# The end of a weight stream: last modes in another bank, last Z in two halves, first U laid later

## The chip, the cores and the metric

The kernel runs on one core of a Trainium2 chip. The metric is the device time of one execution in microseconds (us), the median of several runs. TensorE (PE) multiplies, with its weight loads (PEld) shown apart; VectorE (DVE), ScalarE (ACT) and GpSimd (POOL) work on elements; SyncE (SP), ScalarE and GpSimd issue transfers (DMA). Products land in PSUM, which the program hands out in banks of 512 float32 a partition, and have to be copied to SBUF from there.

## What is computed

Eight batches of 576 positions with eight heads of 64 go through a masked attention (four heads local, four strided). Its result x, of 576 rows by 512 features, goes through a mixing step in the frequency domain and a channel product with a rectifier:

```python
X = np.fft.rfft(x, axis=1)
Xr, Xi = np.real(X[:, :n_modes]), np.imag(X[:, :n_modes])      # n_modes = 64
Yr = np.einsum('bmd,mde->bme', Xr, w_r) - np.einsum('bmd,mde->bme', Xi, w_i)
Yi = np.einsum('bmd,mde->bme', Xr, w_i) + np.einsum('bmd,mde->bme', Xi, w_r)
Y[:, :n_modes] = Yr + 1j * Yi
u = x + np.fft.irfft(Y, n=S, axis=1)
return u + np.maximum(u @ w_ch, 0.0)
```

The weights w_r and w_i are 64 matrices each of 512 by 512 float32. They are by far the most of what is read.

## The kernel before

**Stages.** The program's order is written out by hand: each engine executes its instructions in the order in which the Python code issues them, and the framework adds the waits. First comes the strided half of the attention (up to line 836), then the local half with the first modes (lines 839 to 862), then the rest of the modes of the first half with the channel product of x (lines 893 to 935), then the stage "late" (937 to 1041) and the output stage (1042 to 1082).

**Modes.** A mode m of a half is a 256-row slice of w_r[m] and of w_i[m]: a weight tile of 128 partitions (64 real, 64 imaginary), four row groups c and 512 columns e. `w_fetch` (line 157) fetches two modes at a time through GpSimd's queue, converting float32 to float16. Most pairs are two transfers of 512 KB; the last two pairs are cut by mode, so that each of their transfers carries one mode's real or imaginary half (lines 188 to 190, 256 KB). Each transfer waits for the landing of the eighth transfer before it, and for the modes that held its buffer before.

`mode(slot, m)` (line 614) multiplies. In the last 16 modes (48 to 63 of slot 1) the weights stand still and the spectrum X moves: sixteen small matmuls (line 630, 128x16) a mode, four row groups for each of four column groups e. Eight modes share one PSUM tile `y` (lines 623 and 624). VectorE adds the finished ones to the other half's product Y0 and writes the spectrum tile YT (line 564, `spectrum`): for the last tile after mode 61 (six modes) and after mode 63 (two).

**Between the modes.** In the stage "late", `late[i]` names work that follows the i-th mode of `rest`: `renew` (line 948) adds the inverse transform of the first 96 spectrum rows to v0 (channel product of x) and xo (x itself), through pairs of PSUM banks `p`, three of them in rotation. After mode 62 (`late[22]`, line 1037) come `v_early(0)`, `v_early(1)` and `u_early(0)`: each lays two tiles of v0 or xo into a PSUM pair with a product by the identity `idn` (lines 987 and 992), as the start of an accumulation.

**After the last mode.** Lines 1042 to 1053: `spec_z(3, 0)` multiplies the last 32 spectrum rows (four batches of them) by w_ch into `zp`, four matmuls of 512 columns (line 736); ScalarE copies it to `zzs[0]`; eight transposes give the same rows of Y into `yp`, which VectorE copies to `yys[0]` and `yys[1]`.

**Output stage.** Its 18 items are pairs of output tiles. For item k, `v_early` lays V, `new_rows` (line 1001) adds the last spectrum rows to it, `v_done` (line 1013, ScalarE) takes the Relu into `rl`; `u_early` lays U, `new_rows` adds, and `u_done` (line 1020, VectorE) adds U and `rl` into `osb`, which SP sends out. Item 0 is done in two pieces. The first two items are written out (lines 1056 to 1064); from k = 2 on the loop issues V of item k beside U of item k-1. V, and U of even items, use the pairs `p`; U of odd items the pair `u`. At k = 8 (lines 1066 to 1069) the second half of the last spectrum rows is multiplied into one more of the pairs `p` (`held`) and ScalarE copies it to `zzs[1]`.

## Time and profile before

| | |
|---|---|
| median of three runs | 427.61 us (427.32 to 427.89) |
| profiled execution, span from first to last instruction | 426.7 us |
| PE / PEld busy | 346.4 us (81%) / 208.2 us (49%) |
| DVE / ACT / POOL busy | 234.7 / 218.3 / 110.7 us |
| transfers | 91.62 MB, mean 215 GB/s |
| GpSimd's queue (weights, q, k, v), share of 16 engines' span | 96.2% |
| mean granted TensorE clock | 0.926 |

The profiled execution has no time of its own beside its span; the median of the runs is 0.9 us above it, which is what lies before the first and after the last instruction and the difference between executions.

How to read it: "busy" is the time in which an engine's instructions ran. The page cuts the span into 40 slices and gives for each the busy share of the engines, the granted clock and the transfers' share. The chain that ended last is followed back from the last instruction, at each step to what released it; a stretch of it names what had to be shorter for the end to come earlier. The timeline lists instructions with start, length and, in brackets, how long the engine idled before and what ended that. A matmul's length has a tail in which the next one already runs: matmuls of 512 columns start 0.21 us apart and are listed with 0.38.

### The profile page before, as it was taken

How to read it: one execution, taken by the hardware profiler on the slowest of the kernel's cores; microseconds unless marked ns; L12 is line 12 of the kernel's file. 1: busy time of each engine (PE TensorE's matmuls, PEld its weight loads, DVE VectorE, ACT ScalarE, POOL GpSimd, SP SyncE). 2: the span in 40 equal slices, each digit the busy share in tenths (PEclk: the TensorE clock that was granted, in tenths of full speed). 3: DMA queues.
4: the chain of work that ended last, by engine and by line, in shares of the span. 5: the costliest groups of instructions: out<-in, count | busy, mean ns of one | idle time of the engine just before them, and what ended most of it. 6: DMA issues, size and time to landing. Idle time of an engine off the chain costs nothing.

```text
span 426.7 us, 9768 instructions
## 1 busy us (share of the span) xinstructions
PE 346.4 (81%) x4167; PEld 208.2 (49%) x4167; DVE 234.7 (55%) x466; ACT 218.3 (51%) x390; POOL 110.7 (26%) x196
## 2 busy tenths in 40 slices
PE   2977878769999698889768788878788867889993
PEld 2866767554656365566433344435444423445330
DVE  3788778851355154356113246746676354655884
ACT  1687678643656356556642235423442444443872
POOL 8332333322423222222222322222232222210000
PEclk9999899967999689999995889989999979989997
DMA  8999999999999999999999999999999999995698
GB/s 150 210 212 212 213 213 213 211 211 211 214 213 213 213 213 215 212 214 215 210 214 211 213 214 213 210 213 215 212 213 214 213 213 214 214 212 105 244 355 287
DMA packets 30938, 91.62 MB, mean 215 GB/s; under 512 B 4464, under 2 KB 5232, under 8 KB 30896
## 3 DMA queue, kind: packets, MB, share of 16 engines
q0 software_dynamic: 25168, 81.28, 96.2%
q1 hardware_dynamic: 4976, 9.13, 5.9%
q10 hardware_dynamic: 752, 0.61, 0.5%
q8 instruction: 32, 0.52, 0.5%
q14 instruction: 10, 0.08, 0.0%
HBM read 162.83 MB, written 9.44 MB: 404 GB/s over the span
## 4 chain that ended last, share of the span: by engine, by line
DMA 47%; PE 29%; DVE 14%; ACT 5%; issue 3%; DVEq 0%; POOL 0%; ACTq 0%; POOLq 0%
DMA wt<-in_moe_w_i_dram 38%; DMA wt<-in_moe_w_r_dram 7%; PE y L597 5%; DVE xb L241 3%; DVE kz L283 3%; PE p L987 2%; ACT X L251 2%; PE sc L532 2%; PE tp L413 2%; PE sc L459 1%; PE p L1001 1%; PE y L532 1%; PE p L760 1%; DVE yy L752 1%; DVE rec L240 1%
## 5 line engine op out<-in xcount | busy, mean ns | idle before, releaser
L597 PE MATMUL y<-wt,X 128*32 128x512 f16 (+1 forms) x448 | 70.9, 430 | 20.1 <-DMA wt<-in_moe_w_i_dram 20.1
L186 POOL DMA_DIRECT2D wt<-in_moe_w_r_dram x59 | 34.7, 588 | 126.4 <-PE y L597 56.3
L186 POOL DMA_DIRECT2D wt<-in_moe_w_i_dram x60 | 35.4, 590 | 68.3 <-DMA wt<-in_moe_w_i_dram 44.4
L597 PEld LDWEIGHTS <-X 128*32 128x32 f16 (+1 forms) x448 | 28.1, 140 | 39.4 <-DMA wt<-in_moe_w_i_dram 18.6
L727 DVE COPY xo<-tp 128x512 f16<-128x512 f16 x32 | 22.1, 691 | 36.8 <-PE tp L725 36.8
L726 ACT ACTIVATE v<-sc 128x512 f16<-128x512 f32 x32 | 19.1, 597 | 44.2 <-PE sc L717 44.2
L717 PE MATMUL sc<-w_cp,xT 128*128 128x512 f16 x128 | 36.9, 410 | 1.9 <-DVE xT L690 1.9
L489 ACT ACTIVATE PL<-sc 128x480 f16<-128x480 f32 (+1 forms) x48 | 27.0, 578 | 21.3 <-PE sc L475 21.0
L241 DVE TENSOR_TENSOR xb<-av,rec 90x256 f16<-90x256 f32 (+2 forms) x80 | 36.0, 450 | 2.8
L240 DVE RECIPROCAL rec<-av 90x4 f32<-90x4 f32 (+2 forms) x80 | 14.6, 183 | 39.3 <-PE av L504 28.2
L251 ACT ACTIVATE yr<-y 128x512 f16<-128x512 f32 x28 | 16.7, 597 | 36.8 <-PE y L597 35.6
L961 DVE TENSOR_TENSOR xo<-p,xo 128x1024 f16<-128x1024 f32 x16 | 19.6, 1225 | 21.7 <-PE p L760 21.7
L420 DVE COPY qT<-tp 128x576 f16<-128x576 f16 x16 | 11.9, 752 | 34.7 <-PE tp L413 34.7
L251 ACT ACTIVATE v<-p 128x1024 f16<-128x1024 f32 x16 | 16.4, 1023 | 23.1 <-PE p L760 23.1
L378 ACT ACTIVATE PL<-sc 90x360 f16<-90x360 f32 (+1 forms) x48 | 22.7, 490 | 7.0 <-PE sc L371 6.4
L251 ACT ACTIVATE v<-tp 128x640 f16<-128x640 f16 (+1 forms) x24 | 19.0, 807 | 11.8 <-PE tp L447 9.3
L413 PE MATMUL tp<-cI_s,ring 64*64 64x64 f16 x864 | 22.4, 197 | 2.7 <-DVE qT L420 2.4
L459 PE MATMUL sc<-cMl_s,cI_s 128*128 128x480 f16 (+1 forms) x48 | 19.4, 405 | 4.5 <-ACT PL L489 2.9
L276 PE MATMUL tp<-cI_s,ring 72*128 72x72 f16 x256 | 15.4, 207 | 8.7 <-DMA ring<-in_v_dram 7.1
L413 PEld LDWEIGHTS <-ring 64*64 64x64 f16 x864 | 17.5, 110 | 9.4 <-issue 5.4
L251 ACT ACTIVATE kz<-tp 64x360 f16<-64x360 f16 (+1 forms) x32 | 18.9, 592 | 6.2 <-PE tp L413 5.2
L1013 ACT ACTIVATE rl<-p 128x1024 f32<-128x1024 f32 (+1 forms) x19 | 18.4, 979 | 5.7 <-PE p L1001 3.1
(142 smaller groups left out, 737.9 us busy)
## 6 DMA issues: line engine op xcount, KB each, us to landing
wt<-in_moe_w_i_dram POOLq DMA_DIRECT2D x60, 512.0 KB, 18.8
wt<-in_moe_w_r_dram POOLq DMA_DIRECT2D x59, 512.0 KB, 17.7
out_dram<-osb SPq DMA_DIRECT2D x15, 512.0 KB, 3.4
ring<-in_v_dram POOLq DMA_DIRECT2D x8, 288.0 KB, 13.4
ring<-in_q_dram POOLq DMA_DIRECT2D x8, 288.0 KB, 13.6
ring<-in_k_dram POOLq DMA_DIRECT2D x8, 288.0 KB, 13.1
ring<-in_v_dram POOLq DMA_DIRECT2D x3, 512.0 KB, 14.8
ring<-in_q_dram POOLq DMA_DIRECT2D x3, 512.0 KB, 14.8
```

What stands on the lines that cost most here:

```text
L186: nc.gpsimd.dma_start(dst, rows)
L241: nc.vector.tensor_tensor(out=dst, in0=val.rearrange("p h (q c) -> p h c q", c=4), in1=rec[0:n, 0:pieces] .to_broadcast((n, pieces, 64)) . ...
L251: nc.scalar.activation(out=out, in_=in_, func=ACTF.Copy)
L378: nc.scalar.activation(out=PS[0:n, ds(POFF[t], 4 * n)], in_=scp[0:n, 0 : 4 * n], func=ACTF.Exp, scale=SCALE,)
L413: nc.tensor.transpose(tp[ds(64 * hp, 64), ds(64 * i, 64)], qn[ds(64 * hp, 64), ds(64 * (9 * g + i), 64)], idn[ds(64 * hp, 64), ds(64 * hp, ...
L459: nc.tensor.matmul(scp[:, 0 : n * times].rearrange("p (h x) -> p h x", h=times), idn, mask_rows("cMl", n, times), start=True, stop=False,)
L489: nc.scalar.activation(out=dst, in_=src, func=ACTF.Exp, scale=SCALE)
L597: nc.tensor.matmul(yp[ds(a, 32), :], Xh[half][pr, c].rearrange("p b r (h m) -> p (b r h) m", h=2)[:, :, mm % 32], wt[pr, XC[c], :], start= ...
L717: nc.tensor.matmul(vp, xT[:, ch], w_chs["cp"][:, ch, :], start=(ch == 0), stop=(ch == 3),)
L726: nc.scalar.activation(out=v0, in_=vp, func=ACTF.Copy)
L727: nc.vector.tensor_copy(out=xo.rearrange("p (h q c) -> p h q c", h=2, c=4), in_=tp[:, 0:512].rearrange("p (h c q) -> p h q c", h=2, c=4),)
L961: nc.vector.tensor_tensor(out=xo, in0=up[:, 0:n], in1=xo, op=AluOp.add)
```

## The change

- **Transfers.** The last mode (63) is fetched in four transfers: columns 0 to 1023 of the tile's 2048 (row groups 0 and 1), real and imaginary, then columns 1024 to 2047 (row groups 2 and 3). Each is 128 KB.
- **Bank.** Mode 62 takes a new tile `y`, which modes 62 and 63 share.
- **Last mode by rows.** Mode 63 first opens all its 64 columns with one matmul of the identity by a tile of zeros, then adds its sixteen products sorted by row group: eight that need the first two transfers, eight that need the last two.
- **First V and U.** After mode 62 only `v_early(0)` is left; `v_early(1)` follows mode 63; `u_early(0)` follows the row products of items 0 and 1.
- **Last Z.** The product by w_ch is made in two halves of 256 columns, each in a bank of its own of one pair `p`; ScalarE copies the first, VectorE the second, before the transposes of Y.
- **Pairs.** Instead of a rotating pool of three pairs there are three named ones, and `pair(n)` says which is taken: V by the parity of its item, U of even items the third. `held` at k = 8 and V of item 8 are both `(npair[0] + 0) % 3`. In the row products the order for items 0 and 1 stays; they now stand between the transposes of Y and their copies.

```diff
@@ w_fetch
-                single += [(j, ri, dst[:, j], rows[:, j]) for j in ones]
-            for _, _, to, rows in sorted(single, key=lambda x: x[:2]):
+                for j in ones:
+                    n = 2 * DM if m + j == NM - 1 else 4 * DM
+                    for a in range(0, 4 * DM, n):
+                        single.append(
+                            (j, a, ri, dst[:, j, a : a + n], rows[:, j, a : a + n])
+                        )
+            for *_, to, rows in sorted(single, key=lambda x: x[:3]):
                 nc.gpsimd.dma_start(to, rows)
@@ mode
-        if mi == 0:
+        if mi == 0 or m == NM - 2:
             ypt[slot] = psum("y")
...
-        for e in range(4):
-            for c in range(4):
-                nc.tensor.matmul(
-                    yv[:, mi, e, :],
-                    wt[:, XC[c], ds(128 * e, 128)],
-                    Xh[half][:, c, :, :, m],
-                    start=(c == 0),
-                    stop=(c == 3),
-                )
+        last = m == NM - 1
+        steps = [(e, c) for e in range(4) for c in range(4)]
+        if last:
+            steps.sort(key=lambda x: XC[x[1]] // 2)
+            nc.tensor.matmul(
+                yv[:, mi, :, :],
+                idn,
+                cs["cT"][:, S:640].rearrange("p (e x) -> p e x", e=4),
+                start=True,
+                stop=False,
+            )
+        for i, (e, c) in enumerate(steps):
+            nc.tensor.matmul(
+                yv[:, mi, e, :],
+                wt[:, XC[c], ds(128 * e, 128)],
+                Xh[half][:, c, :, :, m],
+                start=(c == 0 and not last),
+                stop=(i == 15 if last else c == 3),
+            )
@@ the stage "late"
-    psum_pools(p=3)
+    psum_pools(p=1)
+    npair = [0]
+
+    def pair(n=None):
+        if n is None:
+            n = npair[0] % 3
+            npair[0] += 1
+        return pss["p"].tile([128, 2, 512], FP, tag=f"p{n}", name="p")
...
-        vp, up = psum("p", pair=True), psum("p", pair=True)
+        vp, up = pair(), pair()
...
-        vps[k] = psum("p", pair=True)
+        vps[k] = pair((npair[0] + k % 2) % 3)
...
-        ups[k] = psum(("p", "u")[k % 2], pair=True)
+        ups[k] = psum("u", pair=True) if k % 2 else pair((npair[0] + 2) % 3)
...
-    late[22] = [lambda: v_early(0), lambda: v_early(1), lambda: u_early(0)]
+    late[22] = [lambda: v_early(0)]
@@ after the last mode
+    v_early(1)
+    zp = pair((npair[0] + 2) % 3)
+    lhs = YS["YT"][:, :, 3, 0:8, :].rearrange("p e x m -> p e (x m)")
+    for j in range(2):
+        for e in range(4):
+            nc.tensor.matmul(
+                zp[:, j, 0:256],
+                lhs[:, e],
+                w_chs["n"][:, e, ds(256 * j, 256)],
+                start=(e == 0),
+                stop=(e == 3),
+            )
+        (nc.vector.tensor_copy if j else act_copy)(
+            out=zzs[0][:, ds(256 * j, 256)], in_=zp[:, j, 0:256]
+        )
     yctx.close()
     with tc.tile_pool(name="ps_s", bufs=1, space=PSUM) as pss["s"]:
-        zp = pss["s"].tile([128, 512], FP, name="zp")
         yp = pss["s"].tile([128, 2, 512], F16, name="yp")
-        spec_z(3, 0, zp)
-        act_copy(zzs[0], zp)
...
+        for k in range(2):
+            new_rows(k, vps[k], zzs)
+        u_early(0)
         for bq in range(2):
             nc.vector.tensor_copy(out=yys[bq], in_=yp[:, bq])
...
-    for k in range(2):
-        new_rows(k, vps[k], zzs)
@@ output stage
         if k == 8:
-            held = psum("p", pair=True)[:, 0]
+            held = pair((npair[0] + k % 2) % 3)[:, 0]
```

More of the change, by code (lines that the diff above doesn't have):

```diff
@@ L941, in spec_late @@
     def spec_late(mm, kept, eng):
-        up = psum("p", pair=True)
+        up = pair()
         for bq in range(2):
```

## The prediction

> **What bounds the kernel now.** I read the 40 slices first, then the chain that ended last, then the timeline of the last 40 us. In the slices the transfer engines are full nearly all the way, at 210 to 215 GB/s: up to 391 us the kernel waits for weights. So only the last weights and what follows them can be changed by this diff, and that stretch has to be read instruction by instruction. The chain there (start, length, what):

> ```profile
> 357.73 19.38 DMA wt<-in_moe_w_i_dram
> 377.10 0.14 issue
> 377.24 0.64 PE y L630 x16
> ...
> 389.30 0.64 issue
> 389.94 0.56 DVE YT L563
> 390.50 0.04 issue
> 390.54 0.64 PE y L630 x16
> 391.17 0.86 PE p L987 x4
> 392.04 0.43 PE p L992 x2
> 392.47 0.49 PE y L630 x16
> 392.96 0.02 issue
> 392.98 0.30 DVE YT L563
> 393.28 0.05 issue
> 393.33 1.05 PE zp L736 x4
> ...
> 394.45 0.61 ACT zz L251
> 395.06 0.04 issue
> 395.10 0.45 PE p L1001 x4
> 395.55 1.07 ACT rl L1013 x2
> 396.62 0.04 issue
> 396.67 0.59 PE p L987 x2
> ```

> Mode 62 (390.54) waits for VectorE to read the bank it shares with modes 56 to 61; six matmuls (L987, L992) then stand ahead of mode 63; after mode 63 come one addition, the Z product, one ScalarE copy, and the output stage. From 396.67 TensorE is on the chain in nearly every step, 1.30 us for an item, except at item 8. The timeline there:

> ```profile
> 404.05 1.04 PE L736 MATMUL p<-w_ch,YT 128*128 128x512 f16 x4
> 404.16 1.02 ACT L1013 ACTIVATE rl<-p 128x1024 f32<-128x1024 f32 x1 [0.27 <-PE p L1001]
> 405.13 0.60 ACT L251 ACTIVATE zz<-p 128x512 f16<-128x512 f32 x1
> 405.23 0.59 PE L987 MATMUL p<-v,cI_s 128*128 128x512 f16 x2
> 406.72 1.23 DVE L1020 TENSOR_TENSOR osb<-u,rl 128x1024 f32<-128x1024 f32 x1 [1.24 <-PE u L1001]
> ```

> The reader is to see that the copy of the second Z (405.13 to 405.73) runs beside the next item's first matmuls (405.23), and that VectorE then idles 1.24 us: a delay of TensorE here isn't hidden. The output transfers do not hide it either: between 407.6 and 409.2 they fall from about 380 GB/s to 267 and 153, so their queue has run low, and what comes after starts when item 7 is added up. The end moves with that.

> **Part by part.** Times are those of the profiled execution (span 426.7). The median of the three runs is 427.61, 0.9 above the span; I add the difference in span to the median.

> *Mode 62 in a new bank.* Its last predecessor on TensorE ends at 390.04; it starts at 390.54. The 0.50 goes. What is late next is not TensorE.

> *Six early matmuls.* Between modes 62 and 63 stand 0.86 + 0.43 = 1.29 us. Two of six stay (0.43), two move behind mode 63, two (first U) behind the four row products of the first items. Mode 63, at 392.31 now, could begin 0.50 + 0.86 earlier, at 390.95. The added zero matmul of 64 columns costs about 0.03.

> *The last weights.* The four last transfers of before were issued at 375.17, 377.39, 379.88 and 382.31 and landed 13.0, 12.1, 10.8 and 9.6 us later: at 388.2, 389.5, 390.7 and 391.9. Before, the last landing was just hidden. Now it is the bound, for the second half of mode 63 alone: the first half should land near 390.7, eight matmuls run on it at once, and eight wait until 391.9. From landing to first matmul took 0.13 at 377.11/377.24, so they start at 392.04; sixteen took 0.47 to issue and the last one 0.17 more, so eight take 0.24 + 0.17: end 392.45 (before 392.95). The gain that is left is 0.50 of the 1.36.

> *Two more issues, packets of half the size.* Each issue waits for the landing of the eighth transfer before it. The last now waits for the one issued at 367.57, landed 16.9 later, at 384.5; that is 7 us ahead of its data, so POOL's queue isn't late. Packets of 2304 bytes (the loads of 66 to 76 us) ran at 211 GB/s, weights of 4096 at 213: 1% of half a mode's 1.2 us is nothing. Bounds: -0.3 (transfers end on slightly different engines) to +0.4 (a third of the 1.2 us that one transfer takes); I take 0, by the row of 2304 bytes.

> [...]

> *Z by halves.* The addition takes 0.04 + 0.29 (row L563, 128x128): 392.78; product from 392.83; the second pair of V (L987, 0.43), moved here, is laid by 392.7, beside the addition. Four matmuls of 256 columns: three steps of 0.107 and a last of 0.29 (rows of 192 columns 0.27, 512 columns 0.38) = 0.61, and 0.05 to ScalarE: 393.49. Its copy of 256 columns: 0.38 (row L561, 128x256). In the built order of the changed kernel the second half's first matmul waits for that ScalarE copy, and VectorE's copy waits for it too. So nothing overlaps: 393.91 + 0.61 + 0.05, VectorE 256 columns 0.415 (row L563, 128x256): 394.99; row products at 395.04 instead of 395.10. Two copies with a product between them take what one product and one copy took, and another 0.4: of the 0.50 only 0.06 is left.

> [...]

> *First U later.* Before, 395.10 to 396.67 held ScalarE's two first Relus, and TensorE had time over. Now TensorE's own row is longer: four row products, two for U, two rows, two for U, two rows. From the steady stage: row products to the next full matmul 0.32, full to full 0.21, full to row 0.32. So 0.32 + (0.21 + 0.32) + 0.32 + (0.21 + 0.32) + 0.32 = 2.02: item 2 starts at 397.06 instead of 396.67. At item 3 (before 397.58, held by ScalarE) it is 397.06 + 0.53 + 0.31 = 397.90: +0.32, and TensorE keeps it, at 1.30 an item. VectorE (osb from 396.3 instead of 396.16) catches up in its idle 0.28 before item 2.

> *The buffers of the output stage.* The named buffers give item 8 the buffer that has just held the second Z (both are number 0 of three), where the rotation of before gave the next one. The built order has item 8's first matmul wait for the zz copy. It ended at 405.73, the matmul started at 405.23 and would now start at 405.77: +0.54. ScalarE has nothing else to do meanwhile; behind the waiting matmul stand U of item 7 and its addition, for which VectorE already idles. Bounds 0 (if the queue of transfers hid it) and 0.6 (the whole copy); I take 0.54, since the transfers run low just there.

> Sum: -0.50 (left of the front) + 0.44 (Z) + 0.38 (first U) + 0.54 (item 8) = **+0.86**: span 427.5, median 428.5.

> **Rivals.**
> 1. *The weights land earlier*: the last landing, 391.9, is 1.2 after the one before, while in 390.5 to 391.5 the transfer share is only 0.08: about one engine of 16 is late. If cutting the transfers spread that, everything after moves with it. At 391.1 (0.8 earlier) the result is +0.06, 427.7: no longer slower; that is the point from which it decides. For it: the thin tail of the share. Against: the same rows go to the same transfers' order.
> 2. *A wait costs nothing*: were item 8's wait hidden, +0.32, 427.9; were the halves of Z to overlap, VectorE's copy would start 0.43 after ScalarE's, at 393.92, and the row products at 394.37, 0.67 earlier: +0.19, 427.8. Against: both waits are written in the built order.
> 3. *A slow stretch*: TensorE's granted clock was 0.69 in 376 to 380 and 1.00 from 384 to 410. A stretch of that depth and length inside the TensorE-bound output stage would cost 0.31 x 4 = 1.2 more, 429.7; a last landing 0.4 later gives 428.9. For it: twelve of the page's forty clock slices are under 0.9. Against: none fell there before.

> **How the numbers follow.** The forecast has 0.64 (own range 427.9 to 429.1), rival 1 0.12, rival 2 0.09, rival 3 0.12, and 0.03 is left for a gain that I don't see. The bound of 0.2% (0.86 us, about what a measurement of this kernel can tell from no change) is at 428.47, so the forecast lies on it: of its 0.64 I put 0.42 above and 0.22 within. Slower: 0.42 + 0.12 = 0.54. Within: 0.22 + 0.09 + 0.07 = 0.38. Faster: 0.03 + 0.02 + 0.03 = 0.08, the first two where rivals 1 and 2 come with more than their price. The range, 427.2 to 429.5, takes in rivals 1 and 2 and the late landing of 3.

> **What would show it.** After: mode 62 without VectorE's wait; mode 63 in two groups of eight with a DMA wait between; second group near 392.0; a ScalarE wait inside the Z product; VectorE's zz copy ahead of the row products near 395.0; item 2 near 397.1; ScalarE's zz copy releasing L1010 at item 8 with the gap before it longer by about 0.5. Wrong if the halves of Z overlap, if item 8 starts during the zz copy, or if the second half lands far from 391.9.

## The result, and the profile after

The changed kernel takes **430.45 us** (median of 4 executions, 429.41 to 431.11) where the kernel before took 427.64 beside it: 2.8 us longer, a ratio of 1.0058 with an interval of 1.0043 to 1.0074. It is slower, as forecast, but by three times the forecast 0.86 us, and above the top of the range, 429.5. The profiled execution took 431.11, with a span of 428.4 us.

The chain that ended last, of the kernel after (start, length, what), from the last weights on:

```profile
384.24 7.17 DMA wt<-in_moe_w_i_dram
391.41 0.14 issue
391.55 0.40 PE y L645 x8
391.94 0.85 PE p L1010 x2
392.80 0.87 PE p L1070 x4
...
393.69 0.39 ACT zz L256
...
394.12 1.02 PE p L1070 x4
...
395.24 0.44 DVE zz L1077
...
395.71 0.40 PE p L1024 x4
...
397.83 0.54 PE p L1010 x2
...
406.23 0.56 ACT zz L256
...
406.83 0.59 PE p L1010 x2
```

Every step that the prediction names is there. The second half of mode 63 starts 0.14 after the last landing (391.41). ScalarE's copy (393.69) stands inside the Z product (L1070), VectorE's copy behind it, the row products (L1024) begin at 395.71, item 2 (the first L1010 after them that is shown) at 397.83. At item 8 the copy zz of ScalarE (406.23) releases L1010. What the prediction did not have is the length of the steps between: four matmuls of 256 columns take 0.87 and 1.02 us, where it has 0.61, and the pair for V (L1010) takes 0.85, where it has 0.43.

The windows of the same execution tell why (start and end, length, busy time of TensorE, of its weight loads, of VectorE, ScalarE and GpSimd, then the granted clock, the transfer share, GB/s). The windows are laid on the instants at which the granted clock changes:

```profile
388.20:391.70 3.50, 1.79 (x35) 1.19 (x34) 1.23 (x3) 0.57 (x1) 0.00 (x0) 0.99 0.44 80
391.70:395.10 3.40, 2.93 (x20) 1.61 (x18) 0.29 (x1) 0.38 (x1) 0.00 (x0) 0.50 0.00 0
```

From 391.7 to 395.1, just over the Z product, TensorE ran at half its clock. In the 3.4 us before that it was busy for half the time (1.79 of 3.50). The profiled execution of before has the same pattern, but earlier:

```profile
374.20:377.60 3.40, 2.16 (x36) 1.21 (x33) 3.01 (x3) 1.66 (x2) 0.73 (x2) 0.99 1.07 214
377.60:381.00 3.40, 3.40 (x19) 1.16 (x17) 0.53 (x1) 1.02 (x1) 0.82 (x2) 0.50 1.05 211
```

There it fell where transfers were the bound, but it left TensorE behind its data: from 377.24 to 388.77 the chain of before runs through TensorE without a gap. That is how mode 62 and mode 63 came to look as if TensorE set their time. This execution's span was 426.7; the median of the 23 executions of before beside the first experiments is 425.9, and of the 98 executions of before beside all experiments nine are as long as 426.7 or longer.

What made TensorE idle in the changed kernel before 391.7 is seen in its timeline (start, length, engine, line, operation, and in brackets the idle time before it with its releaser):

```profile
389.06 0.64 PE L645 MATMUL y<-X,wt 128*128 128x16 f16 x16 [0.71 <-DMA wt<-in_moe_w_i_dram]
...
390.27 0.40 PE L645 MATMUL y<-X,wt 128*128 128x16 f16 x8
391.55 0.40 PE L645 MATMUL y<-X,wt 128*128 128x16 f16 x8 [0.88 <-DMA wt<-in_moe_w_i_dram]
```

The first wait for weights, 0.71, stands ahead of mode 62 and is no work of the change: e1 below, with the schedule of before, has 0.70 there. The second, 0.88, stands between the halves of mode 63. There the schedule of before has its six early matmuls, and e1 waits only 0.50.

### The profile page after: what moved, and what is told of

Same layout as the page of the kernel before. It is cut to its first block, busy times and chain, and to the rows that moved or that the text cites. A ratio compares the mean times of both kernels' runs of the same rounds, so it can differ in the third digit from the quotient of the medians.

```text
span 428.4 us, 9783 instructions
## 1 busy us (share of the span) xinstructions
PE 348.0 (81%) x4172; PEld 209.6 (49%) x4172; DVE 235.2 (55%) x467; ACT 217.9 (51%) x390; POOL 111.7 (26%) x198
## 4 chain that ended last, share of the span: by engine, by line
DMA 43%; PE 33%; DVE 14%; ACT 5%; issue 3%; POOL 1%; DVEq 0%; POOLq 0%
DMA wt<-in_moe_w_i_dram 30%; DMA wt<-in_moe_w_r_dram 12%; PE y L602 6%; PE sc L732 3%; DVE xb L246 3%; DVE kz L288 2%; ACT X L256 2%; PE p L1010 2%; PE sc L537 2%; PE p L1024 1%; PE tp L418 1%; DMA ring<-in_q_dram 1%; DVE yy L767 1%; PE y L537 1%; DVE rec L245 1%
## 5 line engine op out<-in xcount | busy, mean ns | idle before, releaser
L602 PE MATMUL y<-wt,X 128*32 128x512 f16 (+1 forms) x448 | 69.8, 424 | 18.2 <-DMA wt<-in_moe_w_i_dram 18.0
L984 DVE TENSOR_TENSOR xo<-p,xo 128x1024 f16<-128x1024 f32 x16 | 19.6, 1225 | 16.9 <-PE p L775 16.9
L256 ACT ACTIVATE v<-p 128x1024 f16<-128x1024 f32 x16 | 16.4, 1023 | 18.6 <-PE p L775 18.6
```

The source lines that it names most:

```text
L256: nc.scalar.activation(out=out, in_=in_, func=ACTF.Copy)
L602: nc.tensor.matmul(yp[ds(a, 32), :], Xh[half][pr, c].rearrange("p b r (h m) -> p (b r h) m", h=2)[:, :, mm % 32], wt[pr, XC[c], :], start= ...
L984: nc.vector.tensor_tensor(out=xo, in0=up[:, 0:n], in1=xo, op=AluOp.add)
```

## The experiments

All 12 kernels follow, in the order of the runs. Two theories stood after the first reading. **A, the tail outside the span:** the program has more TensorE instructions than before (the profiles count 5 products and 5 weight loads more, 4172 of each against 4167). In the profiled execution of after one more block of instructions is fetched at about 430.1 us, 1.7 us behind the end of the span:

```profile
q8 instruction: 1, 0.02, 1.3%
```

(queue, packets, MB, share of the transfer engines between 426 and 432 us). If that block costs the difference, the change of schedule doesn't. **B, the clock:** the idle time that the change makes ahead of the Z product halves the clock just there, about 1 us, and the three waits of the prediction make the rest.

### e1, e2: more instructions in the kernel before

```diff
-        for t in range(nt):
+        for t in [0] * (6 * half) + list(range(nt)):   # e2: [0] * (1 * half)
```

Twelve more TensorE instructions in e1, two in e2, early in the kernel, where they repeat transposes.

> The kernel before with the first transposes of line 342 repeated six times near 20 us (12 instructions more on TensorE's queue, one more than the change adds; TensorE waits for weights later, so in the span they should be hidden). Theory A (a 33rd block of instructions of 16 KB is fetched after the last instruction, and the execution ends only behind it): span 426.7 within 0.3, a row of the instruction queue about 2 us behind the span's end, and the time 1.0 to 1.8 above before (428.6 to 429.4). Theory B (the 1 to 1.8 us outside the span are an accident of those executions, the loss lies in the span alone): time as before, 427.6 within 0.3.

> The same with one repetition (2 instructions more, well under the 11 that the change adds to TensorE's queue). Theory A: no 33rd block, time 427.6 within 0.3. Theory B: 427.6 within 0.3 too. A time above 428.3 would say that the repetition itself costs, and spoil the first run's reading.

Measured: e1 428.25, ratio 1.0015 (1.0003 to 1.0027); e2 427.85, 1.0003 (0.9995 to 1.0012); before beside them 427.70. e1 lies between what A and what B expected. In e1's profiled execution the block is there, at 428.1, 2.3 behind the end of a span of 425.8, and 3.2 us of the time lie outside the span, where 9 of its 12 executions have 1.7 to 1.9. So A's fetch is real, and the execution in which it was seen has 1.4 us more outside its span, but most executions don't: the median moves by 0.55, of which 0.2 is in the span.

These two runs gave something else: the front of the kernel before in an execution in which TensorE isn't late. The chain of e1:

```profile
381.66 9.60 DMA wt<-in_moe_w_i_dram
391.26 0.14 issue
391.39 0.65 PE y L630 x16
...
392.42 1.05 PE zp L736 x4
...
394.19 0.45 PE p L1001 x4
...
395.75 0.59 PE p L987 x2
...
404.31 0.59 PE p L987 x2
```

Mode 63 (L630) starts 0.14 after the landing: the last weights were the bound before the change too. From that landing to item 8 (404.31) it is 13.05 us. Its timeline has modes 62 and 63 (388.96 and 391.39) both waiting for weights, and mode 62, in the bank of before, not for VectorE:

```profile
388.96 0.64 PE L630 MATMUL y<-X,wt 128*128 128x16 f16 x16 [0.70 <-DMA wt<-in_moe_w_i_dram]
...
391.39 0.64 PE L630 MATMUL y<-X,wt 128*128 128x16 f16 x16 [0.50 <-DMA wt<-in_moe_w_i_dram]
```

### e3: fewer instructions in the kernel after

```diff
-        for ch in range(4):
+        chs = range(3 if b < 2 and t < 3 else 4)
+        for ch in chs:
...
-                stop=(ch == 3),
+                stop=(ch == chs[-1]),
```

> The changed kernel with 12 instructions fewer on TensorE's queue: in six tiles of the product of x by w_ch (batches 0 and 1, three tiles each) the fourth row group is left out, a stage in which TensorE waits for weights; so part of that product is missing. Theory A: the span stays that of the changed kernel (427.6 to 428.6), no row of the instruction queue behind the end, the time 1 to 1.8 below the changed kernel's: 428.6 to 429.4. Theory B: the time stays at 430.4 within 0.5.

Measured: 430.12, ratio 1.0067 (1.0049 to 1.0085). No block is fetched behind the end, and all six executions have 1.7 to 1.8 outside the span; yet the kernel is as slow. Half clock was granted from 391.7 to 395.1 again. A does not carry the difference.

### e4: the kernel after once more

> The changed kernel again, beside the others on one chip, to see which parts of its profile come again. Theory C (the stretch of half clock in 391.7 to 395.1 was met by chance): half clock falls elsewhere, and the first V pair, Z products and first row products come 1.1 sooner, span near 427.4. Theory D (the change itself brings it on, by what TensorE does before): half clock again in 390 to 396, span near 428.4. Both: the fetch behind the end comes again, time 1.8 to 2.7 above the span.

Measured: 430.47, ratio 1.006 (1.0047 to 1.0072), span 428.2 against 425.9 in the median. Its profiled execution has no fetch behind the end, though both theories expected one. The windows, on its own clock instants:

```profile
388.70:392.10 3.40, 2.16 (x37) 1.37 (x37) 0.86 (x3) 0.00 (x0) 0.00 (x0) 0.99 0.29 53
392.10:395.50 3.40, 2.93 (x17) 1.92 (x16) 0.49 (x2) 0.38 (x1) 0.00 (x0) 0.50 0.00 0
```

Half clock once more, 3.4 us long and over the Z product, though it began 0.4 later. It came in each of the three executions of this schedule that were profiled (after, e3, e4). D holds against C.

### e5: the idle time filled

```diff
+            if last and i == 8:
+                fill(3)
...
+    late[21].append(lambda: fill(3))
```

`fill(3)` is three matmuls of 512 columns into a pair that is free, whose result is not used: ahead of mode 62, and between the halves of mode 63. The rest is the kernel after.

> The changed kernel with six matmuls more (128x512, results thrown away) where TensorE waits for weights: three ahead of mode 62, three between the halves of mode 63. Theory D (TensorE stands idle for half of the 3.4 us before the last weights land, and the clock is halved for the next 3.4 us, in which Z is made): no half clock in 390 to 396, Z's first product 0.66 and its second 0.66 instead of 0.95 and 1.0, row products about 394.5 instead of 395.6, span and time 1.0 to 1.2 below the changed kernel's 430.4: 429.2 to 429.4. Theory C (half clock there has nothing to do with idleness): half clock again, time 430.4 or above.

Measured: 429.30, ratio 1.0034 (1.0021 to 1.0047), before 427.99. Its chain, and then windows over nearly the same times as in after:

```profile
391.39 0.14 issue
391.52 0.40 PE y L647 x8
391.92 0.43 PE p L1012 x2
392.35 0.58 PE p L1079 x4
...
393.39 0.61 PE p L1079 x4
...
394.57 0.40 PE p L1026 x4
...
396.68 0.54 PE p L1012 x2
```

```profile
388.20:391.60 3.40, 2.77 (x38) 1.56 (x37) 1.19 (x3) 0.54 (x1) 0.00 (x0) 1.00 0.44 80
391.60:395.00 3.40, 2.79 (x31) 1.77 (x31) 1.20 (x4) 0.39 (x2) 0.00 (x0) 1.00 0.00 0
```

With useless work in the waits the clock stays full, V takes 0.43 and the halves of Z 0.58 and 0.61, as predicted, and the kernel that does more is about 1.5 us faster against its own before (+1.31, where e4 has +2.77). B holds. What is left, +1.31, is near the sum of the terms of the schedule (+1.25, below).

### e6: e5, with Z in one product and one copy

```diff
-    for j in range(2):
-        for e in range(4):
-            ... zp[:, j, 0:256] ...
+    for e in range(4):
+        ... zp[:, 0] ...
+    act_copy(zzs[0], zp[:, 0])
```

> The same six matmuls, and Z made by one product of 512 columns with one ScalarE copy, in the same pair of banks (U still late). Theory E (the second half of Z waits for the first half's copy, so two halves take 2.21 and one product with one copy 1.77): 0.3 to 0.5 below e5_fill. Rival (the copies on two engines do save something): as e5_fill or above it.

Measured: 429.06, ratio 1.003 (1.0016 to 1.0045). From the start of Z to the row products its profiled execution takes 1.68 us (394.30 to 395.98), e5 2.22 (392.35 to 394.57): the halves cost 0.54 there. In the medians only 0.24 less than e5 in time and 0.6 in span is seen, with intervals that overlap. Its profiled execution, 430.97, had half clock at 377.7 and a TensorE behind its data like that of before, so nothing else is read from it.

### e7: e5, with item 8 in another pair

```diff
             held = pair((npair[0] + k % 2) % 3)[:, 0]
+            npair[0] += 1
```

> The same six matmuls, Z by halves, and at item 8 the pairs of banks go on by one after the second Z, so that item 8's V takes another pair than the one ScalarE is still copying from. Theory F (that wait moves everything behind it, the output transfers too): 0.45 to 0.6 below e5_fill; item 8's first matmul beside the zz copy again. Rival (the queue of output transfers hides it): as e5_fill within 0.15.

Measured: 428.99, ratio 1.0019 (1.001 to 1.0029): 0.31 less than e5 in time (0.45 to 0.6 expected), 0.45 in span. The chain of e7 at item 8, which ScalarE's Relu releases now, and not its copy zz:

```profile
404.29 0.38 PE p L1026 x4
404.67 1.01 ACT rl L1038
405.68 0.04 issue
405.72 0.59 PE p L1012 x2
```

From the row products of item 7 to item 8 it is 1.43, in e5 1.98 (403.70 to 405.68).

### e8, e9: bank and rows kept, the waits filled with V and U

```diff
# both: Z, its copy and first U as before; item 8 as in e7
# e8
+    late[21].append(lambda: v_early(0))       # ahead of mode 62
+            if last and i == 8:               # between the halves
+                v_early(1)
+                u_early(0)
# e9
+    late[21] += [lambda: v_early(0), lambda: v_early(1)]
+    late[22] = [lambda: u_early(0)]
```

> Mode 62 in a bank of its own and mode 63 by rows as in the changed kernel; first V ahead of mode 62, second V and first U between the halves of mode 63 (no thrown-away work); Z by one product and one ScalarE copy in a bank of its own, row products and first U in the order of before; pairs shifted at item 8. By the theories D, E, F together: no half clock, row products near 394.0 when the last weights land at 391.4, time 427.2 to 427.7, at or a little under before (427.7). If one of them is wrong, 428.2 or more.

> As e8_best, but with both first V ahead of mode 62 and first U between modes 62 and 63, so that nothing stands between the halves of mode 63. In e8_best the second half started 1.27 after the first (390.81 and 392.08) because four matmuls stood between, some 0.5 after its weights should have landed. If that took the gain: second half within 0.2 of its landing, time 0.3 to 0.6 under e8_best's distance to before, so 0 to 0.4 under before (faster or same). If the landing itself is what sets all of it: as before within 0.2.

Measured: e8 428.19, ratio 1.0005 (0.9993 to 1.0017); e9 428.09, 1.001 (1.0001 to 1.0018). Neither beats the kernel before, where e8 was expected at or a little under it. The reading of e8 on which e9 rests was wrong: e8's last transfer, issued at 384.78, landed 7.2 later, at 391.94, and the second half starts at 392.08, 0.14 behind it as in the other runs. V and U, done 0.01 before, just filled the wait and cost nothing. The chain of e9:

```profile
391.50 0.14 issue
391.64 0.41 PE y L645 x8
...
392.42 1.05 PE zp L751 x4
...
394.19 0.45 PE p L1024 x4
...
404.32 0.59 PE p L1010 x2
```

From the landing to item 8 it is 12.82, 0.23 less than in e1; e8 has the same 12.82 (391.94 to 404.76). That is all that mode 63 by rows gave, since half of its matmuls come ahead of the landing; and the medians show not even that.

### e10: before, with only V and U moved

```diff
-    late[22] = [lambda: v_early(0), lambda: v_early(1), lambda: u_early(0)]
+    late[22] = [lambda: v_early(0)]
...
+    v_early(1)            # after the last mode
...
+    u_early(0)            # after the first row products
```

> The kernel before with one thing changed: second V laid after mode 63 and first U after the first row products, as in the changed kernel (bank, transfers, Z and item 8 as before). Theory D: with 0.86 us of work less in the 3.4 us before the last weights land, TensorE is busy for half of them, the clock is halved in 391 to 395, Z takes 1.9 to 2.2 instead of 1.77 and the row products wait for transposes at half clock; with 0.4 to 0.5 for first U the time is 1.0 to 1.8 above before. Without half clock (theory C) only the 0.4 to 0.5 for first U remain.

Measured: 428.65, ratio 1.0023 (1.0008 to 1.0038). First U later is there: from the row products (394.09) to item 2 (396.21) 2.12, in e1 1.56. The converse of e5 came only in part: in the profiled execution TensorE waits 1.42 for weights ahead of mode 63, but over the clock's own window it was busy for 0.58 of the time and the clock stayed full. Other executions are up to 3 us longer (spans 426.1 to 429.6; before 425.1 to 427.0), which would fit a clock that halves in some of them; none of those was profiled, so this is not shown.

### e11, e12: before, with the cut transfers alone, and with the named pairs alone

```diff
# e11: the loop of w_fetch as in the change, nothing else
# e12: psum_pools(p=1), pair() and its uses as in the change, nothing else
```

> The kernel before with only the last mode's transfers cut in two (four of 128 KB; mode 63 still waits for all four, so nothing else moves). If cutting costs nothing: last landing as in the other profiles of before and its relatives (391.2 to 391.9), time as before within 0.2. If the smaller transfers end later, which would be why e9_best2 with a chain shorter by 0.25 is no faster: landing and time 0.2 to 0.5 above before.

> The kernel before with only the named pairs of banks, so that V of item 8 takes the pair that ScalarE still copies the second Z from (nothing in front of the output stage changes). Theory F: item 8 starts 0.5 later (its gap behind item 7 grows from 1.4 to 2.0), time 0.45 to 0.6 above before. Rival (output transfers hide it): as before within 0.15.

Measured beside before at 427.97: e11 428.09, ratio 1.0003 (0.9992 to 1.0014); e12 428.28, 1.001 (0.9999 to 1.002). The cut costs nothing that can be seen, and e11's last weights landed at 391.6 (issued 384.0, 7.6 later). e11's profiled execution shows one thing more: half clock from 389.6 to 393.0, with the schedule of before on TensorE. The six early matmuls take 1.71 + 0.85 us there instead of 0.86 + 0.43, and mode 63 starts 0.8 after its weights. So half clock so near the end isn't the change's alone. In e12 item 8 waits as predicted:

```profile
403.56 0.38 PE p L1009 x4
403.94 1.00 ACT rl L1021
404.95 0.55 ACT zz L251
405.50 0.04 issue
405.54 0.59 PE p L995 x2
```

1.98 from the row products of item 7 to item 8; in the chain of before 1.44 (403.79 to 405.23). The time moved by 0.31, with an interval of about -0.04 to 0.86 that holds the whole 0.54 as well.

## Why the prediction was right in four terms and wrong in its sum

Landings of the last weights differ by 0.8 us from execution to execution, as much as a term of the sum. So the profiled executions are best set side by side from that landing on, by the starts in their chains (us; the landings of e8 and before are issue plus time to landing, since the chain doesn't show them; e6 and e11 are left out, since TensorE was behind its weights there):

| kernel | last landing | to the row products | to item 8 | to the end | landing to item 8 |
|---|---|---|---|---|---|
| e1 (schedule of before) | 391.26 | 2.93 | 10.12 | 21.5 | 13.05 |
| e2 (schedule of before) | 391.84 | 2.93 | 10.13 | 21.5 | 13.06 |
| e10 (V, U moved) | 391.16 | 2.93 | 10.57 | 21.6 | 13.50 |
| e12 (pairs) | 391.94 | 2.93 | 10.67 | 21.6 | 13.60 |
| e8 (rows; V, U in the waits) | 391.94 | 2.69 | 10.13 | 21.5 | 12.82 |
| e9 (rows; V, U early) | 391.50 | 2.69 | 10.13 | 21.6 | 12.82 |
| e7 (after, filled, item 8 free) | 391.98 | 3.18 | 10.56 | 21.5 | 13.74 |
| e5 (after, filled) | 391.39 | 3.18 | 11.11 | 21.8 | 14.29 |
| e4 (after) | 391.30 | 4.29 | 11.04 | 21.6 | 15.33 |
| e3 (after, fewer instr.) | 391.20 | 4.27 | 11.05 | 21.5 | 15.32 |
| after | 391.41 | 4.30 | 11.12 | 21.6 | 15.42 |
| before, as profiled | 391.94 | 3.16 | 10.13 | 21.5 | 13.29 |

The columns add up: each part of the change shows in its own column, by the same amount (to 0.1) wherever it is.

- **First U later, +0.38: right.** The third column is 10.12 without and 10.57 with it (e10, e7 alike): 0.45.
- **Item 8's buffer, +0.54: right.** 10.12 to 10.67 (e12), and 10.56 to 11.11 (e7, e5): 0.55. The bound of 0, that output transfers hide it, fell: from item 8 to the end it is 21.5 to 21.6 with the wait and without, and 21.8 in e5. The medians show 0.31 of it, in e12 against before and in e7 against e5; the interval of e12 holds the whole.
- **Z by halves, +0.44: right at full clock.** 2.22 in e5, for a predicted 2.21; e1 has 1.77. The two halves did not overlap (rival 2 fell): in the chain ScalarE's copy of the first stands between the two products in every profiled execution of this schedule. The halves were in different banks; the wait was written by the program (in after, 0.47 us released by ScalarE's copy), and what different banks would allow without it no run here shows.
- **The front, -0.50: wrong.** The step that failed is "Mode 62 ... starts at 390.54. The 0.50 goes", read off one execution whose TensorE was behind since its half clock of 377.6 to 381.0. In e1 mode 62, in the old bank, waits 0.70 for weights and not for VectorE, and in e1, e2, e10 and e12 mode 63 starts 0.13 to 0.14 after its landing. What the rows give from the landing on is 0.20 (e1 landing to Z 1.16, e5 and e7 0.96) to 0.24 (e8, e9). So 0.3 of the 0.50 could not be gained in these executions.
- **The cut, 0: right, and rival 1 fell.** The last weights land at 391.20 to 391.98 with the cut and at 391.16 to 391.94 without. The last two of after, issued with eight in flight at 383.0 and 384.2, landed 0.6 apart, at 390.8 and 391.4.
- **Rival 3 was the case.** Its price was 1.2, the runs have 1.11 (second column, 3.18 to 4.29). But the prediction held it for a chance event, 0.12, with "Against: none fell there before". The step failed there: none fell there in before's profile, where TensorE was busy (2.87 of the 3.40 us from 388.0; 0.73 and 0.75 of the clock's interval in e1 and e2). The change takes four of six matmuls out of that stretch, and TensorE was busy for 0.50 to 0.62 of it in the three profiles with half clock; e5, with the time filled, kept the full clock. The four matmuls alone did not bring it in e10's profile (0.58), so idle time of this size can bring half clock and need not; what tips it is open. The prediction's own steps contain that idle time (first half of mode 63 near 390.7, second at 392.04, nothing between); its price was never asked.

The sum of the terms as measured: -0.20 + 0.45 + 0.45 + 0.55 = +1.25 at full clock (e5: +1.31), and +1.11 for the clock, **+2.36**; the spans of e4 and before differ by 2.3. The times differ by 2.8. The 0.4 to 0.5 between lies outside the span (in the means it is 0.3): of the nine executions of this kernel, six have 1.8 to 1.9 there, and three have 2.1 to 2.8, as e1 has 2.2 to 3.2 in three of its twelve. That the block of theory A does this fits the four profiled executions in which it came behind the end: the later it came, the more lies outside the span (e7 0.5 behind and 1.8 outside, e6 1.0 and 2.3, after 1.7 and 2.7, e1 2.3 and 3.2), and those without it have 1.7 to 2.1. No experiment moved the block alone, so this is not shown. Why it is fetched behind the end in some executions only stays open.

Open too: why e8 and e9, 0.23 shorter in their chains, have medians 0.2 and 0.3 longer than before (in e9 part of it lies outside the span: seven of eleven executions have 1.95 to 2.06 there, the median of before is 1.80); and how often the half clock is absent. One execution each of after and e4 has a span of 427.6 and 427.1, near e5's 427.5, and was not profiled.

## What to carry to other kernels

Before a saving is read off a chain, see whether the profiled execution is an ordinary one, because a wait that exists only in that execution can't be saved. A span above the median is a hint and no more: of the 0.8 us here 0.7 was a later landing (391.94, e1 391.26) and 0.24 the wait (13.29, e1 13.05). What gave it away was half clock 13 us ahead of the critical stretch; another sign was the median only 0.9 above the span, where nearly all other executions have 1.7 to 2.1. When work is moved out of a stretch in which TensorE waits for data, price the idle time that it leaves, by the busy share of the stretch against the clock granted next (here shares of 0.50, 0.55 and 0.62 were followed by half clock, 0.58 in e10 by full); three thrown-away matmuls in each of two gaps paid for themselves by more than 1 us. And set executions side by side from the last event that the change can't move (here the last landing), not from the start of the span.

## What the runs showed of the hardware

**A fetch behind the end.** One more block of instructions, 0.02 MB, came 1.7 us (after) and 2.3 us (e1) behind the span's end, and those two executions had 0.9 and 1.4 us more outside their spans than the usual 1.8. In e6 it came 1.0 us behind the end, with 0.5 more outside, and in e7 0.5 behind, with nothing more.
